# Reordering the transfer queue of a fused attention and mixture-of-experts kernel: constants behind the last pair, weight words kept back until their place is free

## The chip, the core and the metric

The kernel runs on one core of a Trainium2 chip. The metric is the device time of one execution in microseconds (us), lower is better; the median of three runs of the kernel before is 803.4 us (802.47 to 803.9). Engine names are those of the profile: PE does matmuls (PEld loads their weights), DVE, ACT and POOL are the vector, scalar and GpSimd engines, and SP only issues transfers. "SPq" marks a step of SP's own instruction queue.

## The reference

Three layers follow one another. The first is a retention attention without softmax, over B = 4 batches, H = 8 heads, S = 576 positions of width 64:

```python
scores = scale * np.matmul(q, k.transpose(0, 1, 3, 2))
ret = scores * Dmat[None, :, :, :]          # gamma_h ** (i - j) for i >= j, else 0
x = np.matmul(ret, v)                       # -> 2304 tokens of width 512
h = x @ w_in
g = h * (1.0 / (1.0 + np.exp(-1.702 * h)))
x = g @ w_out                               # dense layer, hidden width 2048
```

The third is a layer of eight experts: each token goes to the expert with the largest cosine against `expert_emb`, that expert computes `relu(x @ w1[e]) @ w2[e]`, hidden width 1024, and the row is scaled by its gate. The weights of the dense layer arrive as 64-bit words (float64 in the reference's inputs), and the kernel turns them into pairs of float32 parts itself.

## The kernel before, in words

**Attention.** Two heads make a pair, so there are 16 pairs `bp` (4 batches by 4). A pair is worked off in five chunks (`ch` 0 to 3 of 128 positions, and `ch` 4, the tail of 64). The list `steps` (line 325 and on) orders the 80 chunks; even and odd pairs alternate, so two pairs are under way at a time. This text calls an entry of that list a turn, 0 to 79. The last chunks of pairs 8 to 15 are turns 46, 51, 56, 61, 66, 71, 76 and 79. Turn i first issues the score matmuls of turn i + 2 (`scores`, line 239; DVE multiplies their result by a mask, line 256), then the state update (`state`, line 263: matmuls at line 270, and an ACT copy at line 272 that the next chunk of the same pair reads), then the chunk's output (`chunk`). After a pair's fourth and fifth chunk `keep` stores the result (DVE lines 307 and 304).

**Places and loads.** `qz` and `kv` have NBUF = 4 places each. When a pair's fifth chunk is done, SP issues the load of pair bp + 4 into the same places (`load`, line 208: two `qz` transfers of 144 KB and one `kv` transfer of 832 KB, together 1120 KB). Ten turns later PE issues the first scores of that new pair. POOL scales its keys first (`prep`, line 258, POOL line 261).

**Words and their conversion.** The dense layer needs 16 units of weights. Unit u comes as the tile `wd{u}` of 1024 KB (`load_wd`, line 115, SP line 119). `convert` (line 130) turns it into the two parts: an ACT instruction (`magnitude`, line 138), then DVE lines 153, 155, 158 and 163, an ACT cast (`high`, line 140) and a DVE subtraction (`low`, line 145). `magnitude` and `high` are put into the dictionary `later` and written out when `flush` is called. From turn 51 on each turn of the attention calls `flush()` and pulls about 0.36 us of this DVE work; in the dense layer each step pulls 2.6 us.

**Sixteen places for everything.** A place is a tag `unit0` to `unit15`. Attention holds thirteen of them: `qz` and `kv` the first eight, the mask table `tb` the ninth, `x0f` four more. So `wd0` to `wd2` have free places from the start, `wd3` and `wd4` go where `qz0` and `kv0` lie (free after pair 12, turn 66), `wd5` and `wd6` after pair 13 (turn 71), `wd7` and `wd8` after pair 14.

**One queue.** All these transfers are issued by SP, in the order in which the program writes them. An instruction that waits for its place holds back all behind it. The table `WD_AT` and the conditions `bp == 5` and `bp == 6` (lines 346 to 353) say behind which load the first three words and the constants `c`, its 32 columns of `embt`, and `uf` are issued; `wd3` and later words are issued from `convert` itself (line 165). `uf` is cast into `ub` by DVE at turn 60 (line 355).

**After the attention.** The dense layer goes through its units f = 0 to 15 for blocks 0 and 1 together (`dense1`: 12 matmuls, line 383, then `swish`, lines 405 to 412; `dense2`: 9 matmuls, line 394, two steps behind), then for blocks 2 to 5. The experts follow.

Of the kernel before, what the change touches and what calls it, by code (L numbers as in the profile page):

```python
# [25 lines left out]
NF1 = F1 // P  # L26
# [13 lines left out]
WARM = 34  # L40
HOLD = NF1 - LAG - 1 - KD
STOP = 1000.0
WD_AT = (9, 12, 14)
NWD = 3
NBUF = 4
HELD = 2 * NBUF + 1 + NB - 2
# [15 lines left out]
def retention_moe_kernel(  # L62
# [52 lines left out]
    def load_wd(u):  # L115

        t = unit_tile(f"wd{u}", [P, 2048], I32, HELD + u)
        stg["d", u] = t.rearrange("p (n two) -> p n two", two=2)
        SP.dma_start(t, wd[u].bitcast(I32))

    later = {}

    def flush(*keys):
        for k in keys or list(later):
# [3 lines left out]
    def convert():  # L130

        words = [pool.tile([P, 2, 1024], I32, tag="tab", bufs=2, name=f"ca{k}") for k in range(2)]

        def word(u):
            return words[u % 4 // 2][:, u % 2, :]

        def magnitude(u):
            ACT.activation(word(u).bitcast(F32), stg["d", u][:, :, 1].bitcast(F32), AF.Abs)  # L138

        def high(u):  # L140
            ACT.copy(new_unit(u)[:, 0, :], word(u).bitcast(F32))

        def low(u):
            flush(("high", u))
            DVE.tensor_tensor(units[u][:, 1, :], word(u).bitcast(F32), units[u][:, 0, :].bitcast(F32), ALU.subtract)

        magnitude(0)
        for u in range(NF1):
            a = word(u)
            flush(("mag", u))  # L150
            if u + 1 < NF1:
                later["mag", u + 1] = lambda u=u: magnitude(u + 1)
            DVE.tensor_scalar(a.bitcast(F32), a.bitcast(F32), 2.0**-15, CLAMP_HI, ALU.max, ALU.min)
            yield 0.67
            DVE.tensor_scalar(a, a, 3, 0x3FFFFFF8, ALU.logical_shift_left, ALU.bitwise_and)
            yield 0.67
            d = stg.pop(("d", u))
            DVE.scalar_tensor_tensor(a, d[:, :, 1], -0x40000000, a, ALU.bitwise_and, ALU.bitwise_or)
            yield 1.22
            if u:  # L160
                low(u - 1)
                yield 1.22
            DVE.scalar_tensor_tensor(a, d[:, :, 0], 29, a, ALU.logical_shift_right, ALU.bitwise_or)
            if u + NWD < NF1:
                load_wd(u + NWD)
            later["high", u] = lambda u=u: high(u)
            yield 1.22
        low(u)
        yield 0.1
# [28 lines left out]
    def attention_(psum):  # L198
# [133 lines left out]
        for i, (bp, ch) in enumerate(steps):  # L332
            if ch == 2 and bp + 2 < NBP:
                prep(bp + 2)
            if i + 2 < len(steps):
                scores(i + 2)
            if ch < NCH:
                state(bp, ch)
            chunk(bp, ch)
            if ch >= NCH - 1:  # L340
                keep(bp, ch == NCH)
            if ch == NCH:
                if bp + NBUF < NBP:
                    load(bp + NBUF)

                if bp + NBUF in WD_AT:
                    load_wd(WD_AT.index(bp + NBUF))
                if bp == 5:
                    SP.dma_start(c, cst[:, :CU])
                if bp == 6:  # L350
                    SP.dma_start(c[:, CET : CET + KD * E], embt)
                    uf = pool.tile([P, P], F32, tag="cvb", bufs=1, name="uf")
                    SP.dma_start(uf, cst[:, CU:CSL])
            if i == 60:
                DVE.tensor_copy(ub, uf)
            yield


    x0s = {}
# [314 lines left out]

    bg.append(convert())
    for i, _ in enumerate(attention()):
        if i > 50:
            flush()
            pull(0.36)
    psum = ctx.enter_context(tc.tile_pool(name="psum", bufs=1, space=bass.MemoryType.PSUM, reuse_waits="tile"))  # L680
# [297 lines left out]
```

## Time and profile before

| what | value |
|---|---|
| median of three runs | 803.4 us |
| the profiled execution's own time | 803.7 us |
| its span, first to last instruction | 801.6 us |
| PE busy | 758.8 us (95% of the span) |
| DVE, ACT, POOL busy | 456.9, 307.8, 197.3 us |
| attention | about 8 to 100.3 us of the span |
| dense layer and experts | 100.3 us to the end |

PE is busy nearly all the time, and on the chain of work that ended last it has 71% of the span, the transfers 9%. Busy shares are means over stages: to see what a change in the attention is worth, read the stretch from 38 to 105 us, engine by engine, and ask at every idle stretch of PE what ended last. All times below count from the start of the profiled span.

### The profile page before, as it was taken

How to read it: one execution, taken by the hardware profiler on the slowest of the kernel's cores; microseconds unless marked ns; L12 is line 12 of the kernel's file. 1: busy time of each engine (PE TensorE's matmuls, PEld its weight loads, DVE VectorE, ACT ScalarE, POOL GpSimd, SP SyncE). 2: the span in 40 equal slices, each digit the busy share in tenths (PEclk: the TensorE clock that was granted, in tenths of full speed). 3: DMA queues.
4: the chain of work that ended last, by engine and by line, in shares of the span. 5: the costliest groups of instructions: out<-in, count | busy, mean ns of one | idle time of the engine just before them, and what ended most of it. 6: DMA issues, size and time to landing. Idle time of an engine off the chain costs nothing.

```text
span 801.6 us, 13016 instructions
## 1 busy us (share of the span) xinstructions
PE 758.8 (95%) x4996; PEld 682.0 (85%) x4996; DVE 456.9 (57%) x1000; ACT 307.8 (38%) x572; POOL 197.3 (25%) x189
## 2 busy tenths in 40 slices
PE   7975899999989899999999998999999999999994
PEld 6875799999979798999998987888888888888883
DVE  5655588888538887763783687553534435344310
ACT  2432245445454323323322443433544435444321
POOL 2521000000000221201011123334554545545311
PEclk8998699999999999999999999999999999999998
DMA  9895899301210032003004132454545546455200
GB/s 279 281 300 214 276 399 378 109 0 45 116 50 1 1 119 80 1 0 119 1 1 132 39 108 90 133 162 130 198 146 166 184 132 199 150 173 178 80 31 35
DMA packets 33400, 104.97 MB, mean 131 GB/s; under 512 B 4911, under 2 KB 7855, under 8 KB 31024
## 3 DMA queue, kind: packets, MB, share of 16 engines
q1 hardware_dynamic: 29808, 93.73, 35.3%
q0 software_dynamic: 3232, 9.46, 3.3%
q10 hardware_dynamic: 288, 0.85, 0.4%
q8 instruction: 41, 0.67, 0.3%
q14 instruction: 31, 0.25, 0.1%
HBM read 80.90 MB, written 24.18 MB: 131 GB/s over the span
## 4 chain that ended last, share of the span: by engine, by line
PE 71%; DMA 9%; issue 7%; DVE 6%; ACT 3%; POOL 2%; SPq 1%; POOLq 0%; ACTq 0%; DVEq 0%
PE h L383 21%; PE o L394 21%; PE eo L394 12%; PE eh L383 12%; DMA kv<-att 6%; DVE dj L480 3%; DMA wd<-wd 2%; PE sc L251 1%; PE tp L585 1%; DMA we<-we 1%; DVE unit L180 1%; POOL unit L181 1%; POOL out L424 1%; ACT ej L452 1%; DVE h L407 1%
## 5 line engine op out<-in xcount | busy, mean ns | idle before, releaser
L383 PE MATMUL h<-x,unit 128*128 128x384 f32 x1152 | 218.0, 337 | 3.7 <-DVE x_k L412 2.5
L383 PEld LDWEIGHTS h<-x,unit 128*128 128x128 f32 x1152 | 204.0, 188 | 13.9 <-DVE x_k L412 3.8
L181 POOL TENSOR_TENSOR unit<-we,unit 128x512 fp32r<-128x512 f32 x64 | 104.9, 1646 | 149.4 <-ACT unit L179 149.3
L383 PE MATMUL eh<-xt,unit 128*128 128x352 f32 x672 | 117.1, 323 | 0.0
L383 PEld LDWEIGHTS eh<-xt,unit 128*128 128x128 f32 x672 | 111.0, 188 | 6.3
L480 DVE CUSTOM_DVE_ANT_0 dj<-xr,en 128x512 f32<-128x512 f32 x120 | 92.9, 827 | 1.1 <-ACT xr L464 1.0
L180 DVE TENSOR_TENSOR unit<-we,unit 128x512 fp32r<-128x512 f32 x64 | 58.4, 912 | 41.8 <-ACT unit L179 41.8
L179 ACT CAST unit<-we 128x1024 fp32r<-128x1024 f32 x64 | 66.9, 1048 | 7.7 <-DMA we<-we 7.7
L256 DVE TENSOR_TENSOR pr<-sc,tb 128x256 f32<-128x256 f32 (+1 forms) x80 | 31.3, 395 | 35.5 <-PE sc L251 34.6
L251 PE MATMUL sc<-qz,kv 128*64 128x128 f32 (+1 forms) x512 | 38.5, 273 | 13.4 <-DMA kv<-att 8.9
L251 PEld LDWEIGHTS sc<-qz,kv 128*64 128x64 f32 x512 | 33.3, 156 | 15.5 <-issue 12.4
L272 ACT ACTIVATE kv<-s,tb 128x64 f32<-128x64 f32 x64 | 19.9, 314 | 45.9 <-PE s L270 44.7
L424 POOL DMA_INDIRECT out<-y,idx x24 | 23.6, 982 | 49.2 <-ACT y L594 47.1
L447 POOL TENSOR_TENSOR enrm<-scr,c 128x8 f32<-128x8 f32 x1 | 1.7, 1685 | 131.1 <-ACT ej L452 131.1
L261 POOL TENSOR_TENSOR kv<-kv,tb 128x512 f32<-128x512 f32 x15 | 16.3, 1089 | 64.2 <-DMA kv<-att 57.0
L270 PE MATMUL s<-kv 128*64 128x64 f32 x256 | 21.8, 243 | 8.8 <-ACT kv L272 8.7
L289 PE MATMUL ao<-pr,kv 128*64 128x128 f32 x256 | 29.2, 299 | 0.0
L376 POOL TENSOR_TENSOR x<-x0s,x 128x768 fp32r<-128x768 f32 x3 | 6.0, 1984 | 87.8 <-ACT x L375 87.8
L424 POOL DMA_INDIRECT xs<-xr,slot x18 | 19.0, 1056 | 34.2 <-DVE ov_all L559 16.4
L270 PEld LDWEIGHTS s<-kv 128*64 128x64 f32 x256 | 17.6, 156 | 9.6 <-ACT kv L272 9.4
L138 ACT ACTIVATE ca<-wd 128x1024 f32<-128x1024 f32 x16 | 18.4, 1153 | 10.0 <-DMA wd<-wd 10.0
L286 PE MATMUL ao<-qz,kv 128*64 128x128 f32 x192 | 22.0, 298 | 0.2 <-issue 0.2
(1256 smaller groups left out, 1494.4 us busy)
## 6 DMA issues: line engine op xcount, KB each, us to landing
we<-we SPq DMA_DIRECT2D x64, 512.0 KB, 3.5
wd<-wd SPq DMA_DIRECT2D x16, 1024.0 KB, 10.8
kv<-att SPq DMA_DIRECT2D x15, 832.0 KB, 6.5
xs<-fill SPq DMA_DIRECT2D x22, 257.0 KB, 10.7
xrow<-xr SPq DMA_DIRECT2D x18, 257.0 KB, 4.6
qz<-qt SPq DMA_DIRECT2D x32, 144.0 KB, 4.6
rin<-xs SPq DMA_DIRECT2D x8, 514.0 KB, 4.5
x0d<-x0f SPq DMA_DIRECT2D x4, 768.0 KB, 12.5
```

The costliest lines, as they stand in the source:

```text
L179: ACT.copy(w[:, 0, :], t)
L180: DVE.tensor_tensor(w[:, 1, :512], t[:, :512], w[:, 0, :512].bitcast(F32), ALU.subtract)
L181: POOL.tensor_tensor(w[:, 1, 512:], t[:, 512:], w[:, 0, 512:].bitcast(F32), ALU.subtract)
L251: PE.matmul(sc[64 * i : 64 * i + 64, j, q0:], t[:, k0 : k0 + 64], q[j][:, q0:P], start=True, stop=True)
L256: DVE.tensor_tensor(pr[:, :, :w], sc[:, :, :w], mask[:, :, :w], ALU.mult)
L270: PE.matmul(s[64 * j : 64 * j + 64], t[:, AK + c0 : AK + c0 + 64], t[:, AV + c0 : AV + c0 + 64], start=ch == 0, stop=True, skip_group_chec ...
L286: PE.matmul(o[64 * j : 64 * j + 64], t[:, AS + 64 * (ch - 1) : AS + 64 * ch], qz[bp % NBUF][:, q0 : q0 + n], start=True, stop=False)
L289: PE.matmul(o[64 * j : 64 * j + 64], t[:, v0 : v0 + 64], pr[:, j, :n], start=ch == 0, stop=True)
L383: PE.matmul(h, w[:, a, P * dc : P * (dc + 1)], xt[:, b, dc, :n], start=k == 0, stop=k == len(terms) - 1)
L394: PE.matmul(o, a[:, c0 : c0 + n], w[:, b, 512:], start=first and k == 0, stop=last and k == 2)
L424: i = POOL.indirect_dma_start(out=dst[:, :], out_offset=bass.IndirectOffsetOnAxis(ap=rows, axis=0), in_=src, in_offset=None, bounds_check= ...
L480: DVE.tensor_tensor_reduce(junk, r[:, :D], en[e // 4][:, e % 4, :], 1.0, 0.0, ALU.mult, ALU.add, dots[:, E * k + e : E * k + e + 1])
```

## The change

Five edits. The table `WD_AT` puts `wd0` behind the load of pair 8 instead of 9, `wd1` behind that of pair 11 instead of 12, and `wd2` behind that of pair 15 instead of 14. The constants move from behind the loads of pairs 9 and 10 to behind that of pair 15, and `c` is written in two parts that do not overlap (before, the second transfer into `c` wrote over columns of the first). Words from `wd3` on go into a list `due` and are issued only when the load of pair 15 has been. `later["mag", u + 1]` is set two DVE instructions later. The conversion starts two turns later (`i > 52`), and the cast into `ub` comes after the last turn.

```diff
-WD_AT = (9, 12, 14)
+WD_AT = (8, 11, 15)
@@
+    due = []
+
+    def load_due():
+
+        if st.get("loaded"):
+            while due:
+                load_wd(due.pop(0))
@@ convert
-            if u + 1 < NF1:
-                later["mag", u + 1] = lambda u=u: magnitude(u + 1)
             DVE.tensor_scalar(a.bitcast(F32), a.bitcast(F32), 2.0**-15, CLAMP_HI, ALU.max, ALU.min)
...
             d = stg.pop(("d", u))
+            if u + 1 < NF1:
+                later["mag", u + 1] = lambda u=u: magnitude(u + 1)
             DVE.scalar_tensor_tensor(a, d[:, :, 1], -0x40000000, a, ALU.bitwise_and, ALU.bitwise_or)
...
             if u + NWD < NF1:
-                load_wd(u + NWD)
+                due.append(u + NWD)
+                load_due()
@@ attention_
                 if bp + NBUF in WD_AT:
                     load_wd(WD_AT.index(bp + NBUF))
-                if bp == 5:
-                    SP.dma_start(c, cst[:, :CU])
-                if bp == 6:
+                if bp + NBUF + 1 == NBP:
+
+                    st["loaded"] = True
+                    SP.dma_start(c[:, :CET], cst[:, :CET])
                     SP.dma_start(c[:, CET : CET + KD * E], embt)
                     uf = pool.tile([P, P], F32, tag="cvb", bufs=1, name="uf")
                     SP.dma_start(uf, cst[:, CU:CSL])
-            if i == 60:
-                DVE.tensor_copy(ub, uf)
+                    load_due()
             yield
+        DVE.tensor_copy(ub, uf)
@@
-        if i > 50:
+        if i > 52:
             flush()
             pull(0.36)
```

How the instructions stand. In the rows below a name carries the number of its buffer: `kv3` is the place that pairs 3, 7, 11 and 15 share, `s13` the state of pair 13, `h0` the first hidden block.

SP before, from the load of pair 13 on: two words stand between the loads of pairs 14 and 15, the second of them `wd3`, whose place is `qz0`.

```order
L211 DMA qz1_79<-qt 64x576 x2
L215 DMA kv1_80<-att 128x1664
L211 DMA qz2_81<-qt 64x576 x2
L215 DMA kv2_82<-att 128x1664
L119 DMA wd2_989<-wd 128x2048
L119 DMA wd3_1019<-wd 128x2048
L211 DMA qz3_83<-qt 64x576 x2
L215 DMA kv3_84<-att 128x1664
L119 DMA wd4_1211<-wd 128x2048
```

SP in the changed kernel, the same stretch:

```order
L219 DMA qz1_79<-qt 64x576 x2
L223 DMA kv1_80<-att 128x1664
L219 DMA qz2_81<-qt 64x576 x2
L223 DMA kv2_82<-att 128x1664
L219 DMA qz3_83<-qt 64x576 x2
L223 DMA kv3_84<-att 128x1664
L119 DMA wd2_1053<-wd 128x2048
L358 DMA c_65<-cst 128x174
L359 DMA c_65<-embt 128x32
L361 DMA uf_1057<-cst 128x128
L119 DMA wd3_1059<-wd 128x2048
```

The loads of pairs 13, 14 and 15 now stand in a row; `wd2`, the constants and `wd3` follow.

ACT before, from the first word on; the rows at line 272 are the state copies, those at line 138 read the words `wd1` and `wd2`.

```order
L138 ACTIVATE ca0_915<-wd0_631 128x1024
L272 ACTIVATE kv2_82<-s10_868,tb_85 128x64
L138 ACTIVATE ca0_915<-wd1_846 128x1024
L272 ACTIVATE kv3_84<-s11_941,tb_85 128x64
L272 ACTIVATE kv2_82<-s10_868,tb_85 128x64
L272 ACTIVATE kv3_84<-s11_941,tb_85 128x64 x2
L272 ACTIVATE kv0_78<-s12_1011,tb_85 128x64
L272 ACTIVATE kv3_84<-s11_941,tb_85 128x64
L141 CAST unit0_1033<-ca0_915 128x1024
L272 ACTIVATE kv0_78<-s12_1011,tb_85 128x64 x2
L138 ACTIVATE ca1_916<-wd2_989 128x1024
L272 ACTIVATE kv1_80<-s13_1086,tb_85 128x64
```

ACT in the changed kernel, from the read of `wd1` to that of `wd2`:

```order
L145 ACTIVATE ca0_938<-wd1_775 128x1024
L280 ACTIVATE kv0_78<-s12_1005,tb_85 128x64
L280 ACTIVATE kv3_84<-s11_931,tb_85 128x64
L280 ACTIVATE kv0_78<-s12_1005,tb_85 128x64
L148 CAST unit0_1061<-ca0_938 128x1024
L280 ACTIVATE kv0_78<-s12_1005,tb_85 128x64
L280 ACTIVATE kv1_80<-s13_1083,tb_85 128x64
L280 ACTIVATE kv0_78<-s12_1005,tb_85 128x64
L280 ACTIVATE kv1_80<-s13_1083,tb_85 128x64 x2
L280 ACTIVATE kv2_82<-s14_1150,tb_85 128x64
L145 ACTIVATE ca1_939<-wd2_1053 128x1024
L280 ACTIVATE kv1_80<-s13_1083,tb_85 128x64
```

The read of `wd1` moved from the third chunk of pair 10 to behind the third of pair 11 (turn 57), that of `wd2` from behind the third chunk of pair 12 (turn 62) to behind the first of pair 14 (turn 68).

DVE before, where the dense layer starts; `unit1` is the second part of the unit that the third dense step reads.

```order
L155 TENSOR_SCALAR ca1_916<-ca1_916 128x1024
L307 TENSOR_TENSOR x0f3_89<-ao15_1223,tb_85 128x512
L304 TENSOR_TENSOR x0f3_89<-at15_1287,tb_85 128x64
L158 SCALAR_TENSOR_TENSOR ca1_916<-wd2_989,ca1_916 128x1024
L407 SCALAR_TENSOR_TENSOR g0t_1311<-g0t_1311,h0_1298 128x384
L145 TENSOR_TENSOR unit1_1226<-ca0_915,unit1_1226 128x1024
L163 SCALAR_TENSOR_TENSOR ca1_916<-wd2_989,ca1_916 128x1024
```

DVE in the changed kernel, the same place:

```order
L315 TENSOR_TENSOR x0f3_89<-ao15_1219,tb_85 128x512
L312 TENSOR_TENSOR x0f3_89<-at15_1284,tb_85 128x64
L160 TENSOR_SCALAR ca1_939<-ca1_939 128x1024
L364 CAST ub_66<-uf_1057 128x128
L415 SCALAR_TENSOR_TENSOR g0t_1309<-g0t_1309,h0_1296 128x384
L165 SCALAR_TENSOR_TENSOR ca1_939<-wd2_1053,ca1_939 128x1024
L152 TENSOR_TENSOR unit1_1250<-ca0_938,unit1_1250 128x1024
```

The operation on `wd2` that stood ahead of the first `swish` product `g0t` (line 158 before, 165 after) stands now between it and the subtraction that completes `unit1`.

## Rows read from the trace of the kernel before

**Rows 1.** By stretch: length, PE, PEld, DVE, ACT, POOL busy, clock, DMA share, GB/s.

```profile
200.00:801.00 601.00, 582.61 (x3052) 518.35 (x3051) 315.06 (x754) 226.15 (x411) 170.71 (x153) 1.00 0.31 99
```

**Rows 2.** Who waited for whom, 38 to 101 us: total us, times, longest.

```profile
ACT ca L138 <- DMA wd<-wd: 10.0, 2, 6.6
...
PE s L270 <- ACT kv L272: 8.7, 2, 5.7
PE sc L251 <- DMA kv<-att: 8.3, 4, 3.2
```

**Rows 3.** Busy time by stretch in the attention, columns as in rows 1.

```profile
72.30:77.10 4.80, 4.80 (x114) 4.80 (x110) 4.80 (x12) 1.99 (x5) 1.43 (x1) 0.97 0.90 366
...
80.30:85.90 5.60, 5.60 (x74) 5.60 (x76) 1.90 (x5) 1.07 (x4) 0.00 (x0) 0.50 0.42 142
...
90.70:96.30 5.60, 5.56 (x71) 5.59 (x73) 2.91 (x6) 1.78 (x4) 1.64 (x3) 0.50 0.94 274
```

**Rows 4.** SP's queue in order of time: start, us, line, transfer, count.

```profile
50.39 0.33 SPq L351 DMA_DIRECT2D c<-embt  x1
...
69.22 1.10 SPq L211 DMA_DIRECT2D qz<-qt  x2
...
71.00 11.82 SPq L119 DMA_DIRECT2D wd<-wd  x2
82.88 1.12 SPq L211 DMA_DIRECT2D qz<-qt  x2
```

**Rows 5.** Waits of SP's queue up to 160 us: total us, times, longest.

```profile
SPq L351 <- DMA c<-cst: 6.2, 1, 6.2
```

**Rows 6.** The chain of work that ended last: start, us, what.

```profile
56.00 9.61 DMA wd<-wd
...
71.00 7.86 DMA wd<-wd
...
84.10 6.51 DMA kv<-att
...
90.74 0.87 PE sc L251 x6
...
100.26 6.69 PE h L383 x36
```

**Rows 7.** POOL in order of time: start, us, operation, idle time before it.

```profile
38.01 1.04 POOL L261 TENSOR_TENSOR kv<-kv,tb 128x512 f32<-128x512 f32 x1 [3.68 <-DMA kv<-att]
...
41.32 1.04 POOL L261 TENSOR_TENSOR kv<-kv,tb 128x512 f32<-128x512 f32 x1 [1.72 <-DMA kv<-att]
...
46.48 1.04 POOL L261 TENSOR_TENSOR kv<-kv,tb 128x512 f32<-128x512 f32 x1 [3.56 <-DMA kv<-att]
...
53.59 1.04 POOL L261 TENSOR_TENSOR kv<-kv,tb 128x512 f32<-128x512 f32 x1 [5.51 <-DMA kv<-att]
57.39 1.04 POOL L261 TENSOR_TENSOR kv<-kv,tb 128x512 f32<-128x512 f32 x1 [2.76 <-DMA kv<-att]
```

**Rows 8.** All engines in order of time, 80 to 104 us.

```profile
78.89 1.14 ACT L138 ACTIVATE ca<-wd 128x1024 f32<-128x1024 f32 x1 [3.39 <-DMA wd<-wd]
...
80.27 0.48 PE L270 MATMUL s<-kv 128*64 128x64 f32 x4 [3.03 <-ACT kv L272]
```

**Rows 9.** Groups of instructions, the attention's DVE work: busy, mean ns, idle before.

```profile
L256 DVE TENSOR_TENSOR pr<-sc,tb 128x256 f32<-128x256 f32 (+1 forms) x80 | 31.3, 395 | 35.5 <-PE sc L251 34.6
```

**Rows 10.** The same by form, 56 to 101 us.

```profile
L307 DVE TENSOR_TENSOR x0f<-ao,tb 128x512 f32<-128x512 f32 x7 | 4.8, 687 | 1.6 <-PE ao L289 1.6
```

**Rows 11.** All engines in order of time, start of the dense layer.

```profile
103.64 1.22 DVE L145 TENSOR_TENSOR unit<-ca,unit 128x1024 fp32r<-128x1024 f32 x1
103.76 0.52 ACT L408 CAST g0h<-g0t 128x384 fp32r<-128x384 f32 x1 [0.62 <-DVE g0t L407]
...
104.92 1.72 PEld L383 LDWEIGHTS h<-x,unit 128*128 128x128 f32 x10 [0.20 <-DVE unit L145]
```

**Rows 12.** DVE in order of time, in the middle of blocks 0 and 1.

```profile
153.62 0.56 DVE L407 SCALAR_TENSOR_TENSOR g13t<-g13t,h 128x384 f32<-128x384 f32 x1 [1.42 <-ACT g13t L405]
```

## The prediction

> **What bounds the kernel now.** I read the busy time by stretch first. From 200 us on PE works 582.61 of 601 us at the full clock [rows 1]: nothing of the change reaches that part but the moment at which it starts. So the question is when the dense layer begins, 100.26 us now [rows 6], and whether its first blocks run as they did.
>
> The waits between 38 and 101 us say what delays it [rows 2]. Three kinds: PE waits for a `kv` load (8.3 us in all); PE waits for a state copy on ACT (8.7 us), and ACT was itself held by `magnitude`, which waited for a word (10.0 us, the longest 6.6). After the later of these idle stretches PE runs at half its clock: 5.6 us at 0.50 from 80.3 us, 5.6 us at 0.50 from 90.7 us [rows 3]; each costs half its length, 2.8 us. The idle stretch that ended at 53.59 was not followed by one, since the next five turns took 3.8 us [rows 7], as short as any: an idle PE doesn't always pay it.
>
> SP's queue shows why the loads come late [rows 4]. The write of `embt` into `c` waited 6.2 us for the earlier write into the same tile [rows 5] and went out at 50.39, with the load of pair 11 behind it. At 71.0 two words take 11.82 us to issue: `wd3` waits for pair 12 to end, and the load of pair 15 behind it goes out at 82.88, though its own place came free with pair 11, one pair earlier. That load lands at 90.6 [rows 6], and PE resumes at 90.74.
>
> **The change, part by part: prices first.** POOL starts a pair's `prep` when its `kv` has landed, so its rows date the landings. Between those of pairs 7 and 8, 38.01 and 41.32, lies one load of 1120 KB: 338 KB per us. Between 46.48 and 53.59 lie a word, the 103 KB of `c` and a load, 2247 KB: 316 KB per us [rows 7]. I take 3.5 us for a load and 3.2 for a word, which is the slower of the two rows; the faster gives 3.3 and 3.0. The Trainium skill, "DMA: Bandwidth & Descriptors", section "Bandwidth", measured 341 GB/s for a 1 MB transfer (on another issuing path); an estimate by it is 3.4 and 3.1 us, which the first of these two rows bears out, and the last word would land about 1 us earlier than in my sum.
>
> Five turns cost 3.8 us when fed (53.59 to 57.39 [rows 7]). With the conversion running DVE needs five masks of 0.395 us, 0.69 and about 0.2 us for `keep` and 5 x 0.36 us of conversion, 4.7 us [rows 9, 10]; DVE was indeed busy 4.80 of 4.80 us at 72.3 [rows 3]. So 3.8 us up to turn 52 and 4.8 after it.
>
> **Walking the queue.** `kv8` lands at 41.3 as now. Then, in the new order, if the queue never runs dry: `wd0` 44.5, `kv9` 48.0 (now 46.5), `kv10` 51.5 (now 53.6), `kv11` 55.0, `wd1` 58.2, `kv12` 61.7, `kv13` 65.2, `kv14` 68.7. It doesn't run dry, because each load's places come free in time. PE's side, by the rule that the first scores of a pair stand ten turns behind its load: turn 41 starts at 48.0 (1.5 us later than now), turn 46 at 51.8, turn 51 at 55.6, turn 56 would start at 59.4 and waits for `kv12` until 61.8. Then turns 61 and 66 at 66.6 and 71.4: no load is late there. So of the present waits for loads two remain, about 1.5 and 2.4 us; the one for pair 15 goes away.
>
> `magnitude(1)` stands at turn 57, near 63 us; `wd1` landed at 58: the wait of 6.6 us goes. What is late next is `wd2`. The load of pair 15 is issued after turn 61, at 67.4; `kv` 1.2 us later (82.88 to 84.10 now), `wd2` 0.5 us behind it, at 69.1. The same word took 7.86 us behind a load, `wd1` 9.61 [rows 6]; I take 7.9, since at 69 us only one other load is on its way: `wd2` lands at 77.0. `magnitude(2)` is queued on ACT behind turn 68, at 73.5, so ACT waits 3.5 us there, and behind it the state copy of turn 69, which PE needs in turn 71. From the start of that instruction to PE's resumption were 1.38 us (78.89 to 80.27 [rows 8]), so PE resumes at 78.4, having reached turn 71 at 76.2 or a little earlier.
>
> From there nine turns are left, as there were after 90.74: these took 9.52 us to the first dense matmul [rows 6], with 5.6 us at half clock in them and DVE's conversion too. With the same 9.5 us the dense layer starts at 87.9 instead of 100.26: 12.4 us gained.
>
> **What is given back.** The third dense step reads `unit1`. Already now its weight load waited 0.20 us for the subtraction at line 145 [rows 11]; the new DVE order puts an operation of 1.22 us (as long as line 145's) ahead of it. PE has nothing else to do there, so 1.2 us are lost; no more, because that operation's input, `wd2`, landed long before.
>
> **At nothing.** The moved constants: 167 KB behind `wd2`, in 0.6 us of queue time; `fill` needs `c` only in the dense layer, and `ub` needs `uf` at about 87 us, eight after its landing. If `uf` were late, the cast would stand in front of `g0t` and cost its delay in full. `wd3` and `wd4` are issued after turn 66, some 16 us ahead of the dense layer (now 18), and land near 85; `magnitude(3)` asks for `wd3` about 7 us into the dense layer. The later place of `mag` lets DVE wait for ACT in some dense steps, up to 0.52 + 1.14 us of ACT [rows 11, 8] less the 1.22 of a DVE operation beside it; DVE idles 1.42 us in each pair of steps now [rows 12], which covers it.
>
> **Sum.** -12.4 + 1.2 = -11.2 us. On the profiled span: 801.6 - 11.2 = 790.4; on its own time 803.7: 792.5; the median lies 0.3 us below that execution, 803.4: 792.2 us. Ends for the unknown terms: with the faster rows `wd2` lands 1.5 us earlier; without a half-clock stretch 2.8 us less; `unit1` hidden, 1.2 us less: 786.7. With `wd2` as slow as `wd1` was, 1.7 us more, and `kv8` late because a word is right behind it, about 1 us: 795.
>
> **Rivals.**
> *Half clock after each wait.* Waits of 1.5, 2.4 and 2 us each slow what follows. The first hides in the wait for `kv12`; the second delays the load of pair 15, and so `wd2`, by its 2.8 us. For it: both later stretches of rows 3; against it: the gap before 53.5 us had none. 792.2 + 2.8 = 795.0. The Trainium skill, "TensorE: Matmul & The Clock Gate", section "HAM oscillation — how this bites in real kernels", says that matmul bursts parted by transfer waits can each start at the low clock; rows 3 agree for two gaps.
>
> *DVE becomes the bound.* If no word is waited for, the tail is DVE's: 27 turns from 57.2 us, 0.57 us of attention and 0.36 of conversion each, 25.1 us, then 0.9 to the first matmul: 83.2, 4.7 us better than above: 787.5. For it: DVE full at 72.3 [rows 3]; against: `wd2` must land by about 73.
>
> *The dense blocks pay for the later `mag`.* Place: DVE's first conversion operation of a unit, waiting for ACT. At the full 0.52 + 1.14 = 1.66 us for each of 16 units 26.6 us are lost, 15.4 more than gained: 818.8. It decides at 0.70 us per unit (11.2 / 16), above which the kernel is slower. Against it: the idle 1.42 us [rows 12], and that a 1.22 us operation of DVE runs meanwhile, which leaves 0.44 at most to hide. A half-way case, 0.4 us per unit left open, gives 798.6.
>
> *It doesn't do what it says:* another instruction still holds SP ahead of pair 15, and the queue stays at the present pace. In the rows of the order nothing that waits for pair 12 stands ahead of that load any more. 803.4.
>
> **How the numbers follow.** Forecast, dense layer at about 88 us: 0.62, from 789.5 to 795. Half clock after each wait: 0.14, up to 797. DVE-bound: 0.10, down to 786.8. Dense blocks: half-way 0.06, slower 0.04. No effect: 0.04. The range from 786.8 to 799 takes in all but the last two. A measurement of this kernel tells about 0.2%, 1.6 us, from no change: faster 0.92, same 0.03 (most of "no effect"), slower 0.05.
>
> **What would show it.** Right: SP issues the loads of pairs 13 to 15 as soon as pairs 9 to 11 end, and the wait of the `embt` write is gone; POOL's `prep` of pair 15 starts before 77; ACT has one wait for a word, at `wd2`, of 2 to 5 us; the first dense matmul stands near 88 and its third step has a PE gap of some 1.2 us for `unit1`; behind it every stage keeps its length. Wrong: new waits for `kv9` and `kv12` of 4 us or more, half clock through most of the attention, `wd2` landing after 80, or PE gaps in the dense blocks that name DVE.

## The result, and the profile after

The changed kernel takes 798.2 us (median of 11 executions, 794.6 to 801.4); the kernel before, run beside it, 805.4 us (11 executions, 802.5 to 807.6). The ratio is 0.991 with a 95% interval from 0.9889 to 0.993, or some 7.2 us (5.6 to 8.9). 11.2 us were predicted. The kernel before also stood 2.0 us higher than in the three executions that the prediction had (803.4), so the absolute time is 6.0 us above the predicted 792.2, and 4.0 us of that is gain that didn't come. In the profiled execution the span is 796.0 us (801.6 before).

The chain of work that ended last (start, us, what) has the predicted shape, as against [rows 6]: no load of pair 15 in it, no second word, and one wait for `wd2`.

```profile
55.05 9.33 DMA kv<-att
64.52 0.52 PE sc L259 x6
...
70.80 9.41 DMA wd<-wd
80.24 1.12 ACT ca L145
...
91.42 2.37 PE h L391 x12
...
94.80 1.22 DVE ca L165
96.02 1.15 DVE unit L152
97.21 2.02 PE h L391 x10
99.24 2.08 PE o L402 x9
```

The dense layer (line 391) begins at 91.42 instead of 100.26. Its three first steps then take 7.82 us up to the first `o` instead of 6.69: the wait for `unit1`.

SP's queue (start, us, line, transfer) answers to [rows 4, 5]: nothing waits in front of the load of pair 15 any more, which goes out at 69.00 instead of 82.88; the constants take some 2 us of queue time behind `wd2`, and no write of `embt` waits for the write of `c`.

```profile
69.00 1.12 SPq L219 DMA_DIRECT2D qz<-qt  x2
70.22 0.53 SPq L223 DMA_DIRECT2D kv<-att  x1
70.80 1.15 SPq L119 DMA_DIRECT2D wd<-wd  x1
72.00 0.42 SPq L358 DMA_DIRECT2D c<-cst  x1
72.47 0.95 SPq L359 DMA_DIRECT2D c<-embt  x1
73.46 0.83 SPq L361 DMA_DIRECT2D uf<-cst  x1
74.39 8.08 SPq L119 DMA_DIRECT2D wd<-wd  x3
```

The waits from 38 to 101 us (total us, times, longest), as against [rows 2]: ACT's for words halved, PE's for loads nearly so, and one long wait of PE for a state copy left.

```profile
ACT ca L145 <- DMA wd<-wd: 5.1, 1, 5.1
...
PE sc L259 <- DMA kv<-att: 4.5, 4, 1.9
...
PE at L294 <- ACT kv L280: 4.0, 1, 4.0
```

PE in order of time gives the idle time ahead of each of these (last column), and busy time by stretch (length, busy time of PE, PEld, DVE, ACT, POOL, clock, DMA share, GB/s) shows which was followed by half clock, as in [rows 3]:

```profile
49.49 0.56 PE L259 MATMUL sc<-qz,kv 128*64 128x128 f32 x8 [1.91 <-DMA kv<-att]
...
64.52 0.56 PE L259 MATMUL sc<-qz,kv 128*64 128x128 f32 x8 [1.88 <-DMA kv<-att]
...
81.61 0.49 PE L294 MATMUL at<-qz,kv 128*64 128x64 f32 x4 [3.95 <-ACT kv L280]
```

```profile
50.00:54.00 4.00, 4.00 (x104) 4.00 (x101) 2.94 (x8) 1.67 (x5) 2.11 (x3) 1.00 0.71 211
...
65.00:69.00 4.00, 4.00 (x101) 3.87 (x99) 3.86 (x9) 2.12 (x5) 1.63 (x2) 1.00 0.67 187
...
81.60:86.60 5.00, 4.99 (x65) 4.99 (x67) 1.37 (x4) 1.11 (x4) 0.00 (x0) 0.50 0.97 308
```

Behind the two waits of 1.9 us for pairs 9 and 12 the clock stayed at 1.00; behind the wait of 3.95 us for `wd2`'s copy PE worked at half clock for 5 us. The DMA share of 0.71 and 0.67 in the first two stretches will matter below.

### The profile page after: what moved, and what is told of

It reads as the page before. It is cut to its first block, busy times and chain, and to the rows that moved or that the text cites. A ratio compares the mean times of both kernels' runs of the same rounds, so it can differ in the third digit from the quotient of the medians.

```text
span 796.0 us, 13012 instructions
## 1 busy us (share of the span) xinstructions
PE 755.8 (95%) x4996; PEld 677.6 (85%) x4996; DVE 456.8 (57%) x1000; ACT 307.0 (39%) x572; POOL 197.8 (25%) x189
## 4 chain that ended last, share of the span: by engine, by line
PE 72%; DMA 7%; issue 7%; DVE 7%; ACT 3%; POOL 2%; SPq 0%; POOLq 0%; ACTq 0%; DVEq 0%
PE h L391 21%; PE o L402 21%; PE eo L402 12%; PE eh L391 11%; DMA kv<-att 4%; DVE dj L488 3%; PE sc L259 1%; DMA wd<-wd 1%; PE tp L593 1%; DMA we<-we 1%; DVE unit L188 1%; PE ao L297 1%; POOL out L432 1%; POOL unit L189 1%; DMA tb<-tab 1%
## 5 line engine op out<-in xcount | busy, mean ns | idle before, releaser
L259 PE MATMUL sc<-qz,kv 128*64 128x128 f32 (+1 forms) x512 | 35.7, 257 | 11.6 <-DMA kv<-att 7.6
L259 PEld LDWEIGHTS sc<-qz,kv 128*64 128x64 f32 x512 | 30.5, 144 | 13.8 <-issue 10.5
L152 DVE TENSOR_TENSOR unit<-ca,unit 128x1024 fp32r<-128x1024 f32 x16 | 19.5, 1221 | 2.8 <-ACT unit L148 2.8
```

Source lines behind the costliest of these rows:

```text
L259: PE.matmul(sc[64 * i : 64 * i + 64, j, q0:], t[:, k0 : k0 + 64], q[j][:, q0:P], start=True, stop=True)
```

## The experiments

Twelve kernels were run. This table has all of them; the last column is the start of the first dense `o` in the profiled execution (the moment from which everything is the same work), for which the prediction's number would be 87.9 + 6.7 + 1.2 = 95.8.

| kernel | ratio to before | 95% interval | gain, us | first `o`, us |
|---|---|---|---|---|
| before, and profiled again | 1 | | 0 | 107.0, 106.8 |
| changed | 0.991 | 0.9889–0.993 | 7.2 | 99.2 |
| changed, again | 0.9909 | 0.9882–0.9937 | 7.3 | 96.0 |
| words kept back alone | 0.9971 | 0.9953–0.9989 | 2.3 | 103.9 |
| constants alone | 0.9999 | 0.9982–1.0015 | 0.1 | 106.5 |
| changed, old conversion | 0.9935 | 0.991–0.996 | 5.2 | 100.1 |
| changed, old word places | 0.9871 | 0.9853–0.989 | 10.4 | 98.3 |
| changed, `magnitude(2)` late | 0.988 | 0.9849–0.9912 | 9.7 | 95.7 |
| changed, PE kept busy | 0.9926 | 0.99–0.9953 | 6.0 | 100.6 |
| changed, unit 1 first | 0.9883 | 0.9858–0.9908 | 9.4 | 97.1 |
| late and unit 1 first | 0.984 | 0.9813–0.9868 | 12.9 | 91.8 |
| the same, conversion early | 0.9837 | 0.9815–0.9859 | 13.1 | 93.2 |
| late, unit 1 first, words later | 0.9877 | 0.9848–0.9905 | 9.9 | 95.7 |

(The gain is the ratio's distance from 1 times 805 us.)

### One part alone: the words, the constants

To the kernel before, only this was added: `wd3` and `wd4` wait in a list until the load of pair 15 is issued.

```diff
-                load_wd(u + NWD)
+                due.append(u + NWD)
+                load_due()
...
+                if bp + NBUF + 1 == NBP:
+                    st["loaded"] = True
+                    load_due()
```

> The kernel before with one part of the change alone: wd3 and wd4 are kept back until the load of pair 15 is issued. Constants, the places of wd0 to wd2, the start of the conversion and the order of DVE stay as before. Theory A (the stalls are separate): the load of pair 15 no longer stands behind wd3; PE's wait of 3.2 us for it at turn 71 goes, with the half clock behind it (2.8 us), so about -6 us; the waits of ACT for wd0 and wd1 and the write of embt behind the write of c (6.2 us) stay. So about 797.5 where before is 803.4, ratio 0.9925. Theory B (all of the change's gain is this one stall): as fast as the changed kernel, ratio 0.991, and the other parts are worth nothing. Theory C (the magnitude that waits for a word decides, not the load): -1 us at most, since that wait (6.6 us) is still there.

Measured: 2.3 us (0.9 to 3.8). That is between A and C, and B falls. The trace shows why. The load of pair 15 goes out at 76.45 and nobody waits for it; but ACT's two waits for words are still there, and the second has grown. ACT and PE in order of time:

```profile
82.77 1.12 ACT L145 ACTIVATE ca<-wd 128x1024 f32<-128x1024 f32 x1 [4.98 <-DMA wd<-wd]
```

```profile
69.67 0.48 PE L278 MATMUL s<-kv 128*64 128x64 f32 x4 [5.26 <-ACT kv L280]
...
84.15 0.48 PE L278 MATMUL s<-kv 128*64 128x64 f32 x4 [4.61 <-ACT kv L280]
...
97.22 5.98 PE L394 MATMUL h<-x,unit 128*128 128x384 f32 x32 [0.31 <-DVE x0f L315]
```

From PE's resumption behind `wd2` to the dense layer are 13.1 us (84.15 to 97.22) where [rows 6, 8] had 20.0 (80.27 to 100.26): this is the stall that the edit removes, 6.9 us. But PE resumes 3.9 us later. `wd2` was issued 2.7 us later in this execution (73.67, before 71.00); that isn't the edit's doing, since SP's queue is the same up to there (72.16 and 72.48 in the two other profiles of the old order). And it took 9.1 us instead of 7.9; the load that could now be issued, 2.8 us behind it, was on its way with it. That what is taken from the last stall is partly waited for at the one ahead fits these 1.2 us, and one profile doesn't show more.

Then the constants alone, moved behind the load of pair 15, with the two writes into `c` no longer overlapping:

```diff
-                if bp == 5:
-                    SP.dma_start(c, cst[:, :CU])
-                if bp == 6:
+                if bp + NBUF + 1 == NBP:
+                    SP.dma_start(c[:, :CET], cst[:, :CET])
...
-            if i == 60:
-                DVE.tensor_copy(ub, uf)
             yield
+        DVE.tensor_copy(ub, uf)
```

> The kernel before with the constants alone moved: c, embt and uf are issued behind the load of pair 15, without overlap of the two writes into c, and ub is cast at the end of attention. Words stay where they were, wd3 ahead of the load of pair 15 too. Theory A: the write of embt no longer waits 6.2 us for the write of c, loads 11 and later are issued earlier, but the next stall (load of pair 15 behind wd3, at 82.88 before) depends on pair 12's end; gain 0 to 1.5 us, about 803 where before is 803.4. Theory C (the overlap is a main cause): -3 us or more, since the load of pair 11 and all behind it come up to 6 us earlier.

Measured: nothing (interval from 1.4 us gained to 1.2 us lost). C falls, A's 0 to 1.5 us hold. The overlap's 6.2 us of [rows 5] are gone, and the load of pair 11 goes out at 49.46 (51.29 before); but words, ACT's waits and the stop at `wd3` are as before (PE in order of time):

```profile
81.41 0.34 PE L270 MATMUL s<-kv 128*64 128x64 f32 x4 [3.38 <-ACT kv L272]
...
91.42 0.56 PE L251 MATMUL sc<-qz,kv 128*64 128x128 f32 x8 [3.93 <-DMA kv<-att]
...
99.83 3.39 PE L381 MATMUL h<-x,unit 128*128 128x384 f32 x18 [0.31 <-DVE x0f L307]
```

### Two parts undone: the conversion's place, the words' places

First the changed kernel with the conversion's old start and the old place of `magnitude`:

```diff
+            if u + 1 < NF1:
+                later["mag", u + 1] = lambda u=u: magnitude(u + 1)
             DVE.tensor_scalar(a.bitcast(F32), a.bitcast(F32), 2.0**-15, CLAMP_HI, ALU.max, ALU.min)
...
-            if u + 1 < NF1:
-                later["mag", u + 1] = lambda u=u: magnitude(u + 1)
...
-        if i > 52:
+        if i > 50:
```

> The changed kernel with the conversion's old start (behind turn 50 instead of 52) and the old place of magnitude(u+1) (before the first DVE operation of unit u instead of behind the second); words and constants stay in the new order. Theory A (separate stalls): magnitude(1) asks for wd1 some 3 us earlier, before it has landed, PE idles for it once more, and wd2's wait is as it is now: 2 to 6 us slower than the changed kernel, ratio 0.994 to 0.998. Theory D (the stalls are in series and absorb one another, as the words kept back alone gave only 2.3 of 6 us): what PE waits for wd1 is taken off its wait for wd2, since wd2's load is issued late only if load 15 is; under 2 us, ratio 0.991 to 0.993.

Measured: 0.9935, 2 us slower than the changed kernel, the two intervals overlapping; between A's 0.994 and D's 0.993. Neither mechanism is seen as it was put: `magnitude(1)` waits only 0.71 us for `wd1`, at no cost to PE. What comes earlier is `magnitude(2)`, and it waits for a word that lands no earlier (ACT, then PE, in order of time):

```profile
60.58 1.20 ACT L145 ACTIVATE ca<-wd 128x1024 f32<-128x1024 f32 x1 [0.71 <-DMA wd<-wd]
...
78.20 1.12 ACT L145 ACTIVATE ca<-wd 128x1024 f32<-128x1024 f32 x1 [8.17 <-DMA wd<-wd]
```

```profile
79.58 0.48 PE L278 MATMUL s<-kv 128*64 128x64 f32 x4 [7.80 <-ACT kv L280]
```

Of D it holds that the stall ends when `wd2` has landed: PE resumes at 79.58, as it does in the changed kernel (81.61, and 79.00 in its second profile). But it stops at an earlier turn, and 13.8 us of attention are left behind it instead of 9.8 and 9.2.

Then the changed kernel with the three first words behind the loads of pairs 9, 12 and 14 again:

```diff
-WD_AT = (8, 11, 15)
+WD_AT = (9, 12, 14)
```

> The changed kernel with the first three words at their old places: behind the loads of pairs 9, 12 and 14 instead of 8, 11 and 15. Theory A: wd2 is issued a load earlier, at about 65 us, and lands by 74, so that ACT no longer waits for it behind turn 68 (2.6 to 5.1 us in two profiles of the changed kernel), and wd1, issued a load later, still comes before magnitude(1) at 66; the load of pair 15 lands 3 us later, near 79, and PE waits for it at turn 71 for as long as it now waits for the state copy. So no gain: 0 to 1 us either way, ratio 0.990 to 0.993. Rival (wd2's wait is what is late, and the load of pair 15 has room): 2.5 us faster, ratio 0.988.

Measured: 0.9871, about 3 us faster than the changed kernel (1 to 5 us, from the two intervals). A falls, the rival's 0.988 is met. The profile shows the mechanism that A had named, but not the gain. ACT waits 1.12 us for `wd2`, and PE not at all for its copy; PE's wait for pair 15 is there instead (PE in order of time):

```profile
54.57 0.60 PE L259 MATMUL sc<-qz,kv 128*64 128x128 f32 x8 [3.39 <-DMA kv<-att]
...
81.06 0.56 PE L259 MATMUL sc<-qz,kv 128*64 128x128 f32 x8 [3.15 <-DMA kv<-att]
```

3.15 us stand against the changed kernel's 3.95, 1.79 and 2.60 us (the third from the kernel with unit 1 first, which is the same up to there), and the dense layer begins at 90.5, where theirs begins at 91.4, 88.2 and 90.4. The profiled execution was the slowest of the four, 796.5 us where their median is 795.2. So that the words' new places cost some 3 us is measured; in which wait the other executions have them isn't seen. ACT doesn't wait for `wd1` here either: the later conversion alone removes that wait, as the new places alone do (0.71 us in the kernel above).

### The new wait

If the wait for `wd2` is what is late, it needn't be waited for in the attention at all:

```diff
-            flush()
+            keys = [k for k in later if k != ("mag", 2)]
+            if keys:
+                flush(*keys)
```

> The changed kernel, with magnitude(2) (ACT, which waits for wd2) not queued during attention but only when the conversion of unit 2 begins, in the dense layer's start: ACT has no instruction behind turn 68 that waits for wd2. Theory A (ACT's wait of 5.1 us for wd2 holds the state copies, PE idles 4.0 us and then has half clock for 5.0 us): that wait goes, worth 4.0 + 2.5 = 6.5 us less what DVE or the last load takes its place; 4 to 6.5 us faster than the changed kernel, ratio to before 0.983 to 0.986. Rival (the load of pair 15 lands just behind, at 77.1, or DVE's conversion is the bound): under 1.5 us, ratio 0.989 to 0.991.

Measured: 0.988, about 2.4 us faster than the changed kernel, intervals overlapping, between the two expectations. In the profile the wait is gone, and the chain that ended last runs mostly over DVE from 65.6 to 79.5 us (DVE busy 3.98 of 4.00 us from 66 to 70, 4.00 from 74 to 78; the changed kernel has 3.99 and 4.00 there, and ACT's wait behind). The dense layer begins at 86.3, but its first steps at a low clock (by stretch, columns as above):

```profile
82.00:86.30 4.30, 2.25 (x42) 1.39 (x36) 2.87 (x8) 2.50 (x4) 0.00 (x0) 1.00 1.01 344
86.30:90.20 3.90, 3.88 (x13) 3.88 (x14) 0.84 (x3) 0.00 (x0) 0.00 (x0) 0.56 1.00 422
```

In the last turns, waiting for DVE and ACT, PE worked 2.25 of 4.30 us, and then the clock fell to 0.56 for 3.9 us, 1.7 us lost. In the kernels below with the same late `magnitude(2)` this came back once (0.67 from 88 to 92 us in the last of them) and stayed away twice.

The other way round, the wait was left and PE kept busy with 64 matmuls that nobody uses:

```diff
+            if i == 71:
+                for _ in range(64):
+                    PE.matmul(scs[0][:, 3 * P :], ones, ones, start=True, stop=True)
```

> The changed kernel with 64 added matmuls of 128 columns on constants in turn 71, ahead of the chunk whose state copy waits for wd2: they keep PE busy for some 3.5 us of the 4.0 us in which it idled, and their result is not used. Theory A (the five microseconds at clock 0.50 behind the wait are caused by PE's idling): the clock stays at 1.00 behind turn 71, worth 2.5 us: ratio to before 0.988. Rival (the nine last turns are bound by DVE and ACT, so PE's clock there costs nothing): the clock stays at 1.00 and the time is that of the changed kernel, ratio 0.991, or slower by what the matmuls add.

The clock did stay up (PE in order of time, then by stretch):

```profile
80.62 3.73 PE L349 MATMUL sc<-ones 128*128 128x128 bf16 x64 [0.16 <-DVE pr L264]
...
85.25 0.34 PE L294 MATMUL at<-qz,kv 128*64 128x64 f32 x4 [0.90 <-ACT kv L280]
```

```profile
84.00:88.00 4.00, 3.10 (x74) 2.93 (x73) 1.39 (x5) 2.34 (x6) 0.18 (x1) 1.00 0.88 317
```

and the rest of the attention took 7.5 us (85.25 to 92.77) instead of 9.8 (81.61 to 91.42). The time doesn't show it: 798.3 us, ratio 0.9926, not below the changed kernel's. In this execution PE had waited 3.01 and 3.05 us for the loads of pairs 9 and 12, `wd2` was issued at 74.78 (70.80 in the changed kernel), took 9.1 us and landed late, at 83.8. That the half clock is caused by the idle PE is shown, in one profile; that it costs 2.5 us of the total isn't.

### The exchange in the dense layer's start

```diff
+            if u == 2:
+                low(1)
+                yield 1.22
             DVE.scalar_tensor_tensor(a, d[:, :, 1], -0x40000000, a, ALU.bitwise_and, ALU.bitwise_or)
...
-            if u:
+            if u and u != 2:
```

> The changed kernel with one pair of DVE operations exchanged at the dense layer's start: the subtraction of unit 1 ahead of the third operation of unit 2. PE's wait of 1.0 us in the third dense step for unit 1 goes: 1.0 us faster than the changed kernel (0.9987 of it), at the limit of what can be timed; in the profile the three steps of 12 matmuls take 6.7 us where they took 7.8. Rival (DVE is then late for unit 2 instead): the gap stands one step later and nothing is gained.

In the profile it does what was said: the subtraction (line 152) starts at 93.81, right behind `g0t`, and the three steps run without a gap (PE in order of time):

```profile
90.42 6.67 PE L394 MATMUL h<-x,unit 128*128 128x384 f32 x36 [0.31 <-DVE x0f L318]
```

So the 1.0 to 1.1 us are shown there. The ratio, 0.9883, is 2 us better than the changed kernel's, with intervals that overlap widely; 1 us can't be told in it. With both edits:

> The changed kernel with magnitude(2) queued only when unit 2's conversion begins, and unit 1's subtraction first. The late magnitude alone gave a ratio of 0.988: no wait of ACT for wd2, the dense layer 5.1 us earlier in the profile, but its first twelve matmuls at clock 0.56, since the last turns, then bound by DVE, kept PE busy for only half the time. Theory A: both gains add, ratio 0.9865. Rival (DVE is the bound of the last turns and of the dense start, so its order only moves the gap): 0.988.

Measured: 0.984, 791.7 us; A's 0.9865 lies in the interval, the rival's 0.988 does not. The dense layer begins at 85.07, at full clock, with its three steps in 6.68 us. In its chain `magnitude(2)` (1.05 us from 82.65) and the DVE operation behind it (0.69 us) still stand ahead of the last `keep`, and so of the dense layer; whether these 1.7 us can be moved too wasn't tried.

### What bounds that one

Two more were tried on top of it. In the first the conversion begins six turns earlier, with less per turn:

```diff
-        if i > 52:
-            keys = [k for k in later if k != ("mag", 2)]
+        if i > 46:
+            keys = [k for k in later if k != ("mag", 2) and (k != ("mag", 1) or i > 58)]
...
-            pull(0.36)
+            pull(0.28)
```

> The kernel with magnitude(2) late and unit 1's subtraction first (ratio 0.984), and in addition the conversion begun behind turn 46 instead of 52 at a rate of 0.28 instead of 0.36 us per turn, with magnitude(1) not queued until turn 59, when wd1 has landed. Theory G (DVE is the bound of the turns behind the wait for pair 12, at 0.57 + 0.36 us each): 0.08 us less in each of the 21 turns from 59 on, 1.7 us less in all, ratio 0.982. Rival (the last loads are the bound there, load 15 landing at 76 or later and four and more turns behind it): nothing gained, 0.984.

Measured: 0.9837, the same. Theory G isn't borne out: in its profile PE waits 2.17, 0.57 and 2.16 us for loads and the dense layer begins at 85.9. Read from that one profile, the loads are the bound again where DVE is relieved. In the second, the words `wd0` and `wd1` stand two loads later:

```diff
-WD_AT = (8, 11, 15)
+WD_AT = (10, 13, 15)
...
-            keys = [k for k in later if k != ("mag", 2)]
+            keys = [k for k in later if k != ("mag", 2) and (k != ("mag", 1) or i > 62)]
```

> The kernel with magnitude(2) late and unit 1's subtraction first (ratio 0.984), and in addition wd0 and wd1 two loads later in the queue (behind the loads of pairs 10 and 13 instead of 8 and 11), with magnitude(1) not queued until turn 63. Theory H (up to pair 12 the queue of transfers is the bound, every word ahead of a load costs PE its 3.2 us or what is left of it): the waits for pair 9 (1.6 us), pair 10 (1.0) and pair 12 (1.1 us in that profile, 1.5 to 3.5 in others) shrink or go, and the dense layer begins 1.5 to 3 us earlier: ratio 0.9805 to 0.982. Rival (DVE's conversion and attention are the bound of the turns behind, so that what is saved ahead of turn 53 is waited for there): under 0.8 us, ratio 0.983 to 0.984.

Measured: 0.9877, some 3 us slower than without it, the intervals touching; both expectations missed. PE's waits for loads moved and didn't shrink, 1.48, 3.42 and 1.72 us instead of 1.05, 1.61, 0.98 and 1.13:

```profile
43.94 0.56 PE L262 MATMUL sc<-qz,kv 128*64 128x128 f32 x8 [1.48 <-DMA kv<-att]
...
58.68 0.56 PE L262 MATMUL sc<-qz,kv 128*64 128x128 f32 x8 [3.42 <-DMA kv<-att]
...
74.78 0.56 PE L262 MATMUL sc<-qz,kv 128*64 128x128 f32 x8 [1.72 <-DMA kv<-att]
```

and behind the long one the clock was 0.72 from 60 to 66 us. In these two profiles a word's transfer is waited for wherever it stands, and four short waits cost less than three longer ones.

### The same kernels profiled again

> The changed kernel without any edit, on the same chip as the three that follow, so that they are compared with it and not with its earlier ratio of 0.991. In its first profile the dense layer began at 91.4 us, 3.5 us later than predicted, partly because that execution was already 2.2 us late at the issue of load 8, ahead of any changed instruction, and wd2 took 9.4 us to land where 7.9 was assumed. If that was the chance of one execution, this profile shows load 8 issued near 34 us and the dense layer near 89; if it belongs to the new order, again 35.5 or later and 91. Ratio 0.989 to 0.993.

> The kernel before without any edit, for a second profile. The question is why the gain at the dense layer's start is larger in the profiles (8.8 and 12.1 us in two executions of the changed kernel, 12.4 predicted) than in the times (7.3 us). Theory E: the profiled execution of before was a good one behind the dense layer's start, where its two long gaps of PE, 2.0 us near 224 and 2.5 us near 272, were not followed by low clock, while eight profiles of kernels in the new order or parts of it had a loss of some 1.55 us behind most of these gaps; then a second profile of before shows one or two such losses too, and a span of 802.5 to 804.5 with the dense layer at 100 again. Theory F: the order of the early transfers decides whether the clock falls there; then this profile again shows none, and a span near 801.5.

The changed kernel's second profile shows load 8 issued at 33.65 and the dense layer at 88.15 (predicted 87.9); ACT waited 2.62 us for `wd2` (predicted 3.5) and PE 1.79. PE in order of time:

```profile
48.63 0.77 PE L259 MATMUL sc<-qz,kv 128*64 128x128 f32 x8 [2.14 <-DMA kv<-att]
...
64.08 0.56 PE L259 MATMUL sc<-qz,kv 128*64 128x128 f32 x8 [2.38 <-DMA kv<-att]
...
79.00 0.34 PE L294 MATMUL at<-qz,kv 128*64 128x64 f32 x4 [1.79 <-ACT kv L280]
```

So the first profile's late start was that execution's. But its span is 794.2, not the 792.7 that 88.15 would give with the first profile's 704.6 us from the dense layer to the end. The reason is behind the dense layer's middle, where PE has two long gaps in every kernel, 2.0 us ahead of the `o` that reads `g28l` and 2.5 to 2.8 us behind `dots`. Busy time by stretch around them, before, before again, changed, and changed again, in this order:

```profile
215.00:240.00 25.00, 22.99 (x115) 20.49 (x114) 7.97 (x16) 13.98 (x32) 1.69 (x1) 1.00 0.25 93
268.00:285.00 17.00, 14.46 (x76) 12.80 (x76) 13.33 (x50) 4.44 (x11) 2.21 (x4) 1.00 0.06 21
```

```profile
215.00:240.00 25.00, 23.02 (x115) 20.51 (x114) 8.15 (x16) 13.94 (x32) 1.68 (x1) 1.00 0.24 87
268.00:285.00 17.00, 14.48 (x69) 12.80 (x68) 12.00 (x46) 3.72 (x10) 0.92 (x4) 0.90 0.00 0
```

```profile
208.00:233.00 25.00, 23.01 (x108) 20.45 (x107) 7.70 (x15) 13.49 (x32) 1.68 (x1) 0.93 0.26 92
262.00:279.00 17.00, 14.24 (x74) 12.61 (x74) 13.34 (x50) 4.37 (x11) 2.19 (x4) 1.00 0.05 20
```

```profile
205.00:230.00 25.00, 23.01 (x108) 20.34 (x107) 7.69 (x15) 13.71 (x32) 1.68 (x1) 0.93 0.25 88
260.00:277.00 17.00, 14.23 (x68) 12.65 (x67) 11.93 (x49) 4.24 (x10) 1.89 (x4) 0.90 0.03 13
```

The work is the same, the gaps are the same, and the clock falls behind them in some executions and not in others: the six or seven matmuls fewer in a stretch (108 for 115, 69 for 76, 68 for 74) are a loss of 1.5 to 1.6 us each time, by the times of the same instructions ahead of the gap and behind it. Before lost it at 0 and 1 of its two gaps, the changed kernel at 1 and 2. Theory E is borne out so far, the first profile of before having been a good one. F falls as it was put, since it expected no loss in the second. That the order shifts the odds isn't refuted: over all profiles the kernels in the old order (before twice, constants alone) lost at 1 of 6 gaps, the other eleven at 13 of 22. That may be chance or not; the runs don't settle it.

## Why the prediction was right, and what was mis-sized

**What bounds the kernel, and which stalls go.** Right: SP's long stop at `wd3` and the write of `embt` that waited are gone; the load of pair 15 is issued as soon as its place is free; ACT has one wait for a word, at `wd2`; the two waits for loads that were to remain, of 1.5 and 2.4 us for pairs 9 and 12, took 1.9 and 1.9, and 2.1 and 2.4 us. At the edge: `prep` of pair 15 starts at 77.1 and 75.3 in the two profiles ("before 77"), and ACT's wait took 5.1 and 2.6 us ("2 to 5"). One of the signs of being wrong, "`wd2` landing after 80", was met in the first profile, at 80.2 (77.6 in the second). The five turns of 3.8 us were read from a row of POOL that a landing ended (57.39 [rows 7]); SP's loads of pairs 12 and 13, at 54.23 and 58.03, give the same. The step of `unit1` was foretold at 1.2 us and took 1.0 to 1.1. The constants and their overlap were entered "at nothing", and alone they are worth nothing.

**The walk of the queue was too fast.** This is the step that failed: "It doesn't run dry, because each load's places come free in time." It does run dry, in part. In the three profiles of the changed kernel up to turn 71 (the changed one twice, and the one with unit 1 first) the DMA share between 50 and 54 us is 0.71, 0.81 and 0.66, since the load of pair 11 waits for turn 41, which waits for pair 9. `kv12` lands at 64.4, 63.9 and 65.7 where the walk has 61.7; the load of pair 15 is issued at 69.0, 68.6 and 70.3 instead of 67.4. From `kv9` to `kv12` took 15.0, 15.4 and 16.1 us where the walk has 13.7; the missing share accounts for some 1.2, 0.8 and 1.4 us of that (an estimate: 4 us times what the share lacks), and the rest is open. Part of the lateness stood ahead of the walk: load 8 went out at 35.9 and 35.6 in the first and third of these profiles, 33.7 in the second and in the one that the prediction had. The next terms held in the mean: `wd2` took 9.4, 7.2 and 7.8 us (7.9 assumed), and from PE's resumption to the dense layer were 9.8, 9.2 and 9.1 us (9.5). The dense layer began at 91.4, 88.2 and 90.4, 90.0 in the mean, 2.1 us later than the 87.9 of the sum, which only the best of the three met, with a `wd2` that was faster than assumed. Busy time from 50 to 54 us in the second and third of these profiles (the first's stands above):

```profile
50.00:54.00 4.00, 4.00 (x72) 4.00 (x69) 1.93 (x6) 1.63 (x5) 0.79 (x2) 0.72 0.81 252
```

```profile
50.00:54.00 4.00, 4.00 (x104) 4.00 (x101) 2.74 (x8) 1.67 (x5) 2.12 (x3) 1.00 0.66 201
```

**"Behind it every stage keeps its length" held but for the clock.** In the mean of its two profiles each, the kernel before lost 1.55 us at 0.5 of its late gaps and the changed kernel at 1.5: 1.5 us more. With the 2.1 us above that is 3.6 of the 4.0 us that are missing. The first part is shown in each trace; the second rests on two profiles of each, and whether the order of the transfers has a hand in it is open. The remaining 0.4 us aren't placed. The base of the prediction was the profile of before that had no such loss.

**Luck in the number.** The measured 798.2 us lie outside the 789.5 to 795 that went with the forecast's own mechanism. They lie inside the whole range, up to 799, thanks to the room for the dense blocks' rival (half-way 798.6), which didn't come.

**The parts don't add up the way the sum was written.** Words kept back alone gave 2.3 us and constants alone 0, and the words' new places cost about 3 us when all else is changed; so, by elimination, most of the gain hangs on the words kept back together with what removes the wait for `wd1`. That wait has two cures, the word's new place and the later conversion, and either is enough (0.71 us and none); with neither, in the kernel with the words kept back alone, it is still 5.6 us. No run has the words kept back and the later conversion without the constants, so what these are worth in company is open. The prediction took the new order as one walk and so had the combined effect about right; it entered the place of `wd2` behind the last load as "what is late next", and put no price on the place that it had before.

**The rivals.** *Half clock after each wait* came in part: behind the wait of 2.1 us for pair 9 the changed kernel's second profile has clock 0.72 from 50 to 54 us, 1.1 us lost; its first has 1.00 behind both its waits of 1.9 us. The Trainium skill, "TensorE: Matmul & The Clock Gate", section "HAM oscillation — how this bites in real kernels", has bursts parted by transfer waits start at the low clock; these traces agree in some executions only. *DVE becomes the bound* did not decide here, where the chain goes through `wd2`; once `magnitude(2)` was taken out of the attention the chain went over DVE, and the dense layer began at 86.3 and 85.1, where the rival had worked out 83.2. *The dense blocks pay for the later `mag`* fell: from 100 to 200 us PE is busy for 100.00 of 100.00 us. *It doesn't do what it says* fell with SP's queue.

## What to carry to other kernels

When loads, words and constants share one queue, price a reordering by walking the queue with the moment at which each place comes free, and add the issue of every load that waits for its place (from 69.00 to 70.75 for the last one here); a queue that was only just full in the walk ran dry in the run. After removing the stall that ends last, look at what instruction of an in-order engine still waits for the last transfer to land, and move that instruction: here a `magnitude` queued later and two DVE operations exchanged gave another 5.6 us (791.7 us, ratio 0.984). The transfer can be moved too: the old places of the words gave about 3 us, and no run has these places together with the two other edits. And of a gain of 1% take two profiles of either kernel before telling where it went, since two executions of one kernel began the same layer 3 us apart.

## What the hardware showed that was not expected

The same gap of PE, 2.0 us long, at the same place of the same work, was followed by a low clock in some executions (0.93 over 25 us, 1.55 us lost) and by the full clock in others; so were PE's waits in the attention of 1.8 to 3.5 us (3.52 us with clock 1.00 from 66 to 72 us behind it in the kernel with unit 1 first; 3.39 us with 0.57 from 54.5 to 58.5 us in the one with the old word places; 1.77 us, up to 55.74, with 0.50 from 56.7 to 59.7 us in the one with the words kept back alone). The longer ones, of 3.7 to 7.8 us, were each followed by it.

The clock also fell with no long gap ahead of it: after 4.3 us in which PE worked 2.25 us, in short pieces between waits for DVE and ACT, it was 0.56 for the next 3.9 us.

A word of 1 MB took between 7.2 and 9.4 us from its issue to its landing in the same place of the same kernel.
